# Folding the transforms over d a second time in a spectral filter with a gated MLP on one Trainium2 core

## The chip, the cores and the metric

The kernel runs on one core of a Trainium2 chip. The metric is the device time of one execution in microseconds, lower is better; it is the median over the runs of the same program.

## What is computed

```python
def _A_ref(x, w_r, w_i):                       # x: 1 x 2048 x 576
    X = jnp.fft.rfft2(x, axes=(-2, -1))        # 2048 x 289 complex
    X = X * (w_r + 1j * w_i)
    return jnp.fft.irfft2(X, s=(S, D), axes=(-2, -1))

def _B_ref(x, w_gate, w_up, w_down):           # F = 4608
    g = jnp.einsum("bsd,df->bsf", x, w_gate)
    u = jnp.einsum("bsd,df->bsf", x, w_up)
    return jnp.einsum("bsf,fd->bsd", _sigmoid(g) * u, w_down)

xn = _layernorm(x, axis=-1)
return x + _A_ref(xn, A_w_r, A_w_i) + _B_ref(xn, B_w_gate, B_w_up, B_w_down)
```

Everything is fp32. The change concerns the part `_A_ref`, and in it the transform over d (576 wide) and its inverse.

## The kernel before

TensorE multiplies fp32 operands that are split in two parts, a high and a low one (`split`: ScalarE copies the high part, VectorE subtracts it), as three products: high by high, low by high, high by low. Every product is one instruction that loads 128 columns of weights and streams up to 512 columns past them.

The gated MLP fills the whole time: `unit` and `plain` make the hidden values (`prod`, L636, 7 products of 512 columns per call into the banks `pA`, `pB`, `pE`), and `down` and `seven` multiply them with `w_down` (`po`, L743, and `ps`, L834, six products of 288 columns for half of a pair of banks). VectorE adds `po` and `ps` to the sums `acc` and `qs`. All of the smaller work takes pairs of PSUM banks from one tag, `pp`, with two buffers.

The spectral part is cut in three phases of 16 pieces, which run as generators beside the second half of the MLP: `begin` says at which step (one call of `prod` of the second pass) a piece starts, and at each step every active piece goes on to its next `yield`.

- `phase1b(t)`, begun every 4.1 steps from step 0, is the transform over d and the first half of that over the rows. Its 128 rows come transposed as `xs`, both halves of d in 2 x 3 blocks of 128 rows: two blocks of 128 and one with the last 32 rows four times. VectorE folds d once: the second half of d is stored backwards, and `eo` holds the differences (L465) and, after the mean is taken off (L466), the sums (L467) of the two halves, 288 values each. ScalarE makes the high parts `fh` (L470), VectorE the low ones `fl` (L471) and those of the last 32 rows, which lie in a part of `fh` (L473). Two steps later come the products `pd`: for sums and differences seven each, of 290 columns (`NQ`; L483). `ah` and `al` are the two parts of `pd`, and `pa` are the next products.
- `phase2(i)` multiplies by the filter.
- `phase3(t)` goes back: products `py`, transposes `pz` (six, of 128 columns), and the inverse transform over d, `pe`, again seven products for each half, of 288 columns (L594). VectorE adds the sum and the difference of the two halves of `pe` to the two halves of a row of the output (L598 to L601).

The products of the transform over d, before:

```python
for e in range(2):
    steps = []
    for k in range(2):
        steps += [(fh[:, e, k, :], cf[:, e, k, :]), (fl[:, e, k, :], cf[:, e, k, :]), (fh[:, e, k, :], cf[:, e, 2 + k, :])]
    steps.append((fh[:KR, e, KT, :], cf[:KR, e, 4, :]))
    for n, (l, r) in enumerate(steps):
        nc.tensor.matmul(pd[:, e, :NQ], l, r, start=n == 0, stop=n == len(steps) - 1)
```

A scheduler orders the instructions of each engine before the run, so this order is fixed; those marked with `keep_in_program_order` or `placed` are held to the order of the program.

Of the kernel before, what the change touches and what calls it, by code (L numbers as in the profile page):

```python
# [9 lines left out]
F32 = mybir.dt.float32  # L10
# [3 lines left out]
OP = mybir.AluOpType  # L14
# [10 lines left out]
FR = HD + 1 - 2 * P  # L25
# [18 lines left out]
KOF = np.array(list(range(1, 257)) + [0] + list(range(257, 289)))  # L44
# [19 lines left out]
def _constants():  # L64
    out = {}

    mid = np.arange(HD) - (D - 1) / 2
    ang = 2 * np.pi * mid[:, None] * KOF[None, :] / D
    t = np.zeros((P, 2, 5, NQ), np.float32)
    for e, v in ((0, np.cos(ang)), (1, -np.sin(ang))):  # L70
        m = np.zeros((HD, NQ))
        m[:, :KD] = v
        m[:, KD - 1 if e == 0 else KT * P] = 0.0
        hi, lo = _split(m)
        for part, w in ((0, hi), (1, lo)):
            t[:, e, 2 * part] = w[:P]
            t[:, e, 2 * part + 1] = w[P:2 * P]
        t[:KR, e, 4] = np.concatenate([hi[2 * P:], hi[2 * P:], lo[2 * P:]])
    out["cf"] = t.reshape(P, 10 * NQ)
# [26 lines left out]

    a = np.where((KOF == 0) | (KOF == HD), 1.0, 2.0)[:, None] / (D * S)
    co, si = a * np.cos(ang.T), a * np.sin(ang.T)
    co[KD - 1] = 0.0
    si[KT * P] = 0.0  # L110
    t = np.zeros((P, 2, 5, HD), np.float32)
    for e, m in ((0, co), (1, si)):
        hi, lo = _split(m)
        for part, w in ((0, hi), (1, lo)):
            t[:, e, 2 * part] = w[:P]
            t[:, e, 2 * part + 1] = w[P:2 * P]
        t[:3 * FR, e, 4] = np.concatenate([hi[2 * P:], hi[2 * P:], lo[2 * P:]])
    out["di"] = t.reshape(P, 10 * HD)
# [4 lines left out]
COLS = np.concatenate([np.arange(HD), np.arange(HD, D)[::-1]])  # L123
# [3 lines left out]
def _layout(x, w_r, w_i, w_gate, w_up, w_down):  # L127
# [4 lines left out]
    v = np.stack([w_r, w_i])[:, :, KOF].reshape(2, N1, N2 // 2, 2, KD).transpose(2, 1, 0, 3, 4)  # L132
    v = np.broadcast_to(v[:, None], (N2 // 2, 2, N1, 2, 2, KD))
    x = x.reshape(S, D)[ROWS][:, COLS]
    xt = x.reshape(NT, P, 2, HD)[..., ks].reshape(NT, P, 2, KT + 1, P).transpose(0, 4, 2, 3, 1)
    xg = xt[TPP:].reshape(2, TPC, P, 2, KT + 1, P).transpose(0, 3, 2, 4, 1, 5).reshape(2, 2, P, (KT + 1) * CW)
    lay = {"x": x.reshape(NT, P, D), "xt": xt.reshape(NT, P, 2 * (KT + 1) * P), "xg": xg, "ri": v.reshape(N2 // 2, P, 4 * KD),
# [11 lines left out]
def spectral_glu_kernel(ctx: ExitStack, tc: tile.TileContext, x, xt, xg, ri, w_in, w_down, out):  # L149
# [302 lines left out]
    def phase1b(t):  # L452
        pool, cf = R["pool"], R["cf"]
        xs = pool.tile([P, 2, KT + 1, P], F32, tag="xs", name=f"xs{t}", bufs=2)
        nc.sync.dma_start(xs.rearrange("p h k s -> p (h k s)"), xt[t])
# [769 lines left out]
```

## Time and profile before

| | us |
|---|---|
| median of 3 runs (1419.65 to 1420.62) | 1419.71 |
| the profiled execution | 1421.62 |
| its span, first to last instruction | 1419.8 |
| TensorE busy with products | 1405.9 (99%) |
| weight loads, which overlap the products | 1235.9 (87%) |
| VectorE busy | 1112.5 (78%) |
| ScalarE busy | 640.6 (45%) |
| mean granted clock of TensorE | 0.997 |

Busy time is a union over the span. A product's own duration in the trace runs from its start until its last result is out, and the next one begins well before that; what a product costs in a stream is the distance from one to the next, which the chain of waits shows as the time of a group divided by its count.

### The profile page before, as it was taken

What the parts mean: (1) busy time and instruction counts of PE and PEld (TensorE: products, weight loads), DVE (VectorE), ACT (ScalarE), POOL (GpSimd) and SP (SyncE); (2) the same over time, 40 slices, a digit from 0 to 9 for tenths busy, and PEclk for the clock granted to TensorE, in tenths of its full rate; (3) what the DMA queues carried; (4) which work ended last, traced back from release to release, by engine and by line L of the source; (5) the groups of instructions that cost most, each with busy time, mean ns of one, the idle gap of its engine ahead of it and who ended that gap; (6) DMA issues with size and microseconds to landing.
All of it is one profiled execution on the core that took longest, in us unless ns stands there. A gap on an engine that the chain in (4) does not pass through costs nothing. (4 is left out here: it accounts for less than half of the span.)

```text
span 1419.8 us, 20725 instructions
## 1 busy us (share of the span) xinstructions
PE 1405.9 (99%) x7883; PEld 1235.9 (87%) x7883; DVE 1112.5 (78%) x1722; ACT 640.6 (45%) x1035; POOL 3.3 (0%) x5
## 2 busy tenths in 40 slices
PE   8999999999999999999999999999999999999998
PEld 6888888888888888888888888888888889999897
DVE  6988888888888888789466888877878877766784
ACT  5644444444444443444235444434545534434431
POOL 0000000000000000000000000000000000000000
PEclk9999999999999999999999999999999999999999
DMA  6498677777777776675767777778888787766643
GB/s 250 181 329 308 256 267 262 270 263 270 263 269 263 269 263 247 242 254 176 270 217 234 224 234 223 217 245 267 275 269 272 236 290 221 247 215 204 195 126 84
DMA packets 130899, 343.10 MB, mean 242 GB/s; under 512 B 12176, under 2 KB 51632, under 8 KB 125936
## 3 DMA queue, kind: packets, MB, share of 16 engines
q1 hardware_dynamic: 129872, 340.47, 71.0%
q8 instruction: 62, 1.02, 0.3%
q10 hardware_dynamic: 928, 1.31, 0.3%
q14 instruction: 37, 0.30, 0.1%
HBM read 205.60 MB, written 136.13 MB: 241 GB/s over the span
## 5 line engine op out<-in xcount | busy, mean ns | idle before, releaser
L636 PE MATMUL pB<-X,w 128*128 128x512 f32 x1484 | 379.9, 393 | 0.0
L636 PEld LDWEIGHTS pB<-X,w 128*128 128x128 f32 x1484 | 268.0, 188 | 49.6 <-ACT v L700 1.3
L636 PE MATMUL pE<-X,w 128*128 128x512 f32 x1064 | 271.8, 392 | 0.5 <-DVE y L701 0.5
L636 PE MATMUL pA<-X,w 128*128 128x512 f32 x1008 | 261.4, 395 | 1.2 <-DVE X L445 0.8
L636 PEld LDWEIGHTS pE<-X,w 128*128 128x128 f32 x1064 | 193.2, 188 | 35.4 <-DVE y L701 1.0
L636 PEld LDWEIGHTS pA<-X,w 128*128 128x128 f32 x1008 | 184.5, 190 | 35.4 <-DVE X L445 1.7
L743 PE MATMUL po<-wd,hh 128*128 128x288 f32 x1216 | 210.8, 295 | 0.0
L834 PEld LDWEIGHTS ps<-wf,hs 128*128 128x128 f32 x1260 | 188.9, 188 | 17.9 <-ACT qs L842 0.9
L834 PE MATMUL ps<-wf,hs 128*128 128x288 f32 x1260 | 202.0, 295 | 0.4 <-ACT qs L842 0.4
L743 PEld LDWEIGHTS po<-wd,hh 128*128 128x128 f32 x1216 | 184.2, 188 | 11.8 <-ACT hh L726 0.4
L747 DVE TENSOR_TENSOR acc<-acc,po 128x576 f32<-128x576 f32 x168 | 125.7, 749 | 67.3 <-PE po L743 66.8
L240 ACT ACTIVATE w<-raw 128x768 fp32r<-128x768 f32 (+1 forms) x106 | 100.8, 952 | 93.1 <-PE pE L636 36.5
L743 PE MATMUL po<-wd,hl 128*128 128x288 f32 x608 | 128.7, 293 | 0.0
L844 DVE TENSOR_TENSOR qs<-qs,ps 128x576 f32<-128x576 f32 x112 | 84.1, 751 | 28.4 <-PE ps L834 27.4
L743 PEld LDWEIGHTS po<-wd,hl 128*128 128x128 f32 x608 | 98.7, 189 | 0.0
L701 DVE TENSOR_TENSOR y<-v,pE 128x512 f32<-128x512 f32 x68 | 46.7, 686 | 52.2 <-ACT v L700 51.3
L844 DVE TENSOR_TENSOR acc<-acc,ps 128x576 f32<-128x576 f32 x90 | 67.5, 750 | 23.3 <-PE ps L834 22.6
L242 DVE TENSOR_TENSOR w<-raw,w 128x512 fp32r<-128x512 f32 (+1 forms) x106 | 81.8, 772 | 3.2 <-ACT w L240 2.9
L721 DVE TENSOR_TENSOR y<-y,g 128x1024 f32<-128x1024 f32 x67 | 81.9, 1222 | 3.1
L770 ACT ACTIVATE hs<-y 128x512 fp32r<-128x512 f32 x105 | 64.8, 628 | 38.2 <-DVE y L721 14.6
L704 ACT ACTIVATE g<-pB 128x512 f32<-128x512 f32 x68 | 40.7, 598 | 89.9 <-PE pB L636 89.9
L700 ACT ACTIVATE v<-pB 128x512 f32<-128x512 f32 x68 | 40.6, 598 | 71.0 <-PE pB L636 70.7
(175 smaller groups left out, 1609.0 us busy)
## 6 DMA issues: line engine op xcount, KB each, us to landing
w<-wsp SPq DMA_DIRECT2D x246, 320.0 KB, 3.5
wsp<-w SPq DMA_DIRECT2D x34, 2240.0 KB, 7.8
raw<-in_w SPq DMA_DIRECT2D x34, 768.0 KB, 9.7
wdsp<-wd SPq DMA_DIRECT2D x36, 576.0 KB, 4.6
wf<-tsp SPq DMA_DIRECT2D x60, 288.0 KB, 3.9
wf<-wdsp SPq DMA_DIRECT2D x45, 288.0 KB, 3.9
std<-in_wd SPq DMA_DIRECT2D x36, 288.0 KB, 5.5
ri<-in_ri SPq DMA_DIRECT2D x16, 578.0 KB, 5.3
```

What stands on the lines that cost most here:

```text
L240: placed(nc.scalar.activation(o[:, :, :3, :], src, AF.Copy))
L242: placed(nc.vector.tensor_tensor(o[:, :, 3:, :], src[:, :, :KT, :], f32(o[:, :, :KT, :]), op=OP.subtract))
L636: nc.tensor.matmul(bank, w[:, sw, :], X[:, x, sx, :], start=start and j == 0, stop=stop and j == len(STEPS) - 1, skip_group_check=skip)
L700: nc.scalar.activation(v[:, 1], bank["B"], AF.Copy)
L701: nc.vector.tensor_tensor(y[:, 1], v[:, 1], bank["E"], op=OP.add)
L704: nc.scalar.activation(g[:, 1], bank["B"], AF.Sigmoid)
L721: nc.vector.tensor_tensor(y, y, g, op=OP.mult)
L743: nc.tensor.matmul(pd[:, b, :HD], h[i], w[k][b], start=g == 0 and n == 0, stop=g == G - 1 and n == 2)
L747: nc.vector.tensor_tensor(a, a, pd[:, :, :HD], op=OP.add)
L770: nc.scalar.activation(hs[:, 0], src, AF.Copy)
L834: nc.tensor.matmul(pd[:, i, :HD], h[:, a, m], w[:, b], start=q == 0, stop=q == 2)
L844: nc.vector.tensor_tensor(o, o, pd[:, :, :HD], op=OP.add)
```

## The change

The transform over d is folded a second time. With the first fold, sums serve the cosines and differences the sines. Now each of them is folded again about the middle of its half: sums and differences of quarters of d (144 values) serve even and odd frequencies apart. The columns of d are ordered by quarters (`COLS`), the frequencies by odd ones first (`KOF`), and they are padded from 289 to 290 with one empty frequency.

In `phase1b`, `xs` comes as 2 x 2 x 2 blocks (the last 16 rows of a quarter eight times), the first fold works on 512 columns instead of 384, and six instructions of 128 columns make the second one, two of them with a sign per partition, `sg`. The products have one quarter each: per half, one product of 290 columns for the remainders of both quarters and six of 144 or 146 columns. ScalarE's high parts and VectorE's low ones cover as many elements as before.

In `phase3` the products `pe` have the same form, one of 288 columns and six of 144, and VectorE joins the quarters with five instructions instead of four. The tables `cf` and `di` shrink, to 128 x 1740 for `cf` from 128 x 2900.

```diff
-        eo = pool.tile([P, 2, KT + 1, P], F32, tag="eo", name=f"eo{t}")
-        tc.keep_in_program_order(nc.vector.tensor_tensor(eo[:, 1], xs[:, 0], xs[:, 1], op=OP.subtract))
-        nc.vector.scalar_tensor_tensor(xs[:, 0], mb.unsqueeze(1).to_broadcast([P, KT + 1, P]), -2.0, xs[:, 0], op0=OP.mult, op1=OP.add)
-        nc.vector.tensor_tensor(eo[:, 0], xs[:, 0], xs[:, 1], op=OP.add)
-        fh = pool.tile([P, 2, KT + 1, P], F32R, tag="fh", name=f"fh{t}")
-        fl = pool.tile([P, 2, KT, P], F32R, tag="fl", name=f"fl{t}")
+        od = pool.tile([P, 2, 2 * P], F32, tag="od", name=f"od{t}")
+        tc.keep_in_program_order(nc.vector.tensor_tensor(od, xs[:, 0], xs[:, 1], op=OP.subtract))
+        ev = xs[:, 0].rearrange("p j (k s) -> p (j k) s", s=P)
+        nc.vector.scalar_tensor_tensor(ev, mb.unsqueeze(1).to_broadcast([P, 4, P]), -2.0, ev, op0=OP.mult, op1=OP.add)
+        nc.vector.tensor_tensor(xs[:, 0], xs[:, 0], xs[:, 1], op=OP.add)
+        eo = pool.tile([P, 2, 3, P], F32, tag="eo", name=f"eo{t}")
+        for e, v in ((0, xs[:, 0]), (1, od)):
+            for c, op in ((1 - e, OP.add), (e, OP.subtract)):
+                nc.vector.tensor_tensor(eo[:, e, c], v[:, 0, :P], v[:, 1, :P], op=op)
+            nc.vector.scalar_tensor_tensor(eo[:, e, 2], v[:, 1, P:], sg, v[:, 0, P:], op0=OP.mult, op1=OP.add)
+        fh = pool.tile([P, 2, 3, P], F32R, tag="fh", name=f"fh{t}")
+        fl = pool.tile([P, 2, 2, P], F32R, tag="fl", name=f"fl{t}")
         nc.scalar.activation(fh, eo, AF.Copy)
...
         pd = pair(f"pd{t}")
         for e in range(2):
-            steps = []
-            for k in range(2):
-                steps += [(fh[:, e, k, :], cf[:, e, k, :]), (fl[:, e, k, :], cf[:, e, k, :]), (fh[:, e, k, :], cf[:, e, 2 + k, :])]
-            steps.append((fh[:KR, e, KT, :], cf[:KR, e, 4, :]))
-            for n, (l, r) in enumerate(steps):
-                nc.tensor.matmul(pd[:, e, :NQ], l, r, start=n == 0, stop=n == len(steps) - 1)
+            nc.tensor.matmul(pd[:, e, :NQ], fh[:KR, e, 2, :], cf[:KR, e, 2, :], start=True, stop=False, skip_group_check=True)
+            for c, o in ((0, slice(0, HQ)), (1, slice(HQ, NQ))):
+                for n, (v, i) in enumerate(((fh, 0), (fl, 0), (fh, 1))):
+                    nc.tensor.matmul(pd[:, e, o], v[:, e, c, :], cf[:, e, i, o], start=False, stop=n == 2, skip_group_check=True)
...
         pe = pair(f"pe{t}")
         for e in range(2):
-            steps = []
+            nc.tensor.matmul(pe[:, e, :HD], zr[:3 * FR, e, :], dr[:3 * FR, e, :], start=True, stop=False, skip_group_check=True)
             for k in range(2):
-                steps += [(zh[:, k, e, :], di[:, e, k, :]), (zl[:, k, e, :], di[:, e, k, :]), (zh[:, k, e, :], di[:, e, 2 + k, :])]
-            steps.append((zr[:3 * FR, e, :], di[:3 * FR, e, 4, :]))
-            for n, (l, r) in enumerate(steps):
-                nc.tensor.matmul(pe[:, e, :HD], l, r, start=n == 0, stop=n == len(steps) - 1)
+                o = pe[:, e, (k + 1 + e) % 2 * HQ:((k + 1 + e) % 2 + 1) * HQ]
+                for n, (l, i) in enumerate(((zh, 0), (zl, 0), (zh, 1))):
+                    nc.tensor.matmul(o, l[:, k, e, :], di[:, e, k, i, :], start=False, stop=n == 2, skip_group_check=True)
         od = pool.tile([P, HD], F32, tag="od", name=f"od{t}")
         nc.scalar.activation(od, pe[:, 1, :HD], AF.Copy)
-        lo, up = a[:, :HD], a[:, HD:]
-        nc.vector.tensor_tensor(lo, lo, od, op=OP.subtract)
-        nc.vector.tensor_tensor(lo, lo, pe[:, 0, :HD], op=OP.add)
-        nc.vector.tensor_tensor(up, up, od, op=OP.add)
-        nc.vector.tensor_tensor(up, up, pe[:, 0, :HD], op=OP.add)
+        V = pool.tile([P, 2, 2, HQ], F32, tag="ev", name=f"ev{t}")
+        for i, op in ((0, OP.add), (1, OP.subtract)):
+            nc.vector.tensor_tensor(V[:, i].rearrange("p a q -> p (a q)"), pe[:, 0, :HD], od, op=op)
+        w = a.rearrange("p (s v q) -> p s v q", s=2, v=2)
+        nc.vector.tensor_tensor(w, w, V[:, :, 0].unsqueeze(1).to_broadcast([P, 2, 2, HQ]), op=OP.add)
+        for i, op in ((0, OP.add), (1, OP.subtract)):
+            nc.vector.tensor_tensor(w[:, i], w[:, i], V[:, :, 1], op=op)
```

The scheduler's order of TensorE at tile 4 of the first transform, in the kernel before, from the second half of `ps2_0` into `pd4` (a name's number counts tiles, and `ps2_1_0` is the first half of the second product of round 2):

```order
L834 MATMUL ps2_0_1_7007<-wf2_0_6832,hs2_0_6900 128x288 x6
L636 MATMUL pB42_6950<-X_66,w38_6102 128x512 x7
L834 MATMUL ps2_1_0_7025<-wf2_1_6898,hs2_1_6971 128x288 x6
L483 MATMUL pd4_7038<-cf_6396,fh4_6989 128x290
L636 MATMUL pA42_6949<-X_66,w38_6102 128x512 x3
L483 MATMUL pd4_7038<-cf_6396,fl4_6990 128x290
L483 MATMUL pd4_7038<-cf_6396,fh4_6989 128x290 x2
L483 MATMUL pd4_7038<-cf_6396,fl4_6990 128x290
L483 MATMUL pd4_7038<-cf_6396,fh4_6989 128x290 x3
L483 MATMUL pd4_7038<-cf_6396,fl4_6990 128x290
```

The same place in the changed kernel:

```order
L853 MATMUL ps2_0_1_7044<-wf2_0_6855,hs2_0_6930 128x288 x6
L655 MATMUL pB42_6980<-X_66,w38_6102 128x512 x7
L853 MATMUL ps2_1_0_7062<-wf2_1_6928,hs2_1_7001 128x288 x6
L655 MATMUL pA42_6979<-X_66,w38_6102 128x512 x7
L655 MATMUL pB42_6980<-X_66,w38_6102 128x512 x3
L495 MATMUL pd4_7075<-cf_6396,fh4_7026 128x290
L498 MATMUL pd4_7075<-cf_6396,fh4_7026 128x144
L498 MATMUL pd4_7075<-cf_6396,fl4_7027 128x144
L498 MATMUL pd4_7075<-cf_6396,fh4_7026 128x144
L498 MATMUL pd4_7075<-cf_6396,fh4_7026 128x146
L498 MATMUL pd4_7075<-cf_6396,fl4_7027 128x146
L498 MATMUL pd4_7075<-cf_6396,fh4_7026 128x146
```

The products `pd4` have moved behind seven products of `pA42` and three of `pB42`, and their first one now reads the remainder rows, which are made last. The second half of `pd4` repeats this form.

VectorE at the same tile, before:

```order
L844 TENSOR_TENSOR qs_6448<-qs_6448,ps2_0_0_6962 128x576
L465 TENSOR_TENSOR eo4_6985<-xs4_6858 128x384
L771 TENSOR_TENSOR hs2_1_6971<-y41_6729,hs2_1_6971 128x512
L466 SCALAR_TENSOR_TENSOR xs4_6858<-mb4_6860,xs4_6858 128x384
L771 TENSOR_TENSOR hs2_2_7034<-y41_6729,hs2_2_7034 128x512
L467 TENSOR_TENSOR eo4_6985<-xs4_6858 128x384
L844 TENSOR_TENSOR qs_6448<-qs_6448,ps2_0_1_7007 128x576
L808 TENSOR_TENSOR y41_6729<-y40_6482,y41_6729 128x512
L471 TENSOR_TENSOR fl4_6990<-eo4_6985,fh4_6989 128x512
L473 TENSOR_TENSOR fh4_6989<-eo4_6985,fh4_6989 32x2x128
L844 TENSOR_TENSOR acc_163<-acc_163,ps2_1_0_7025 128x2x288
```

And in the changed kernel:

```order
L863 TENSOR_TENSOR qs_6450<-qs_6450,ps2_0_0_6992 128x576
L476 TENSOR_TENSOR od4_7015<-xs4_6888 128x512
L790 TENSOR_TENSOR hs2_1_7001<-y41_6752,hs2_1_7001 128x512
L478 SCALAR_TENSOR_TENSOR xs4_6888<-mb4_6890,xs4_6888 128x512
L483 TENSOR_TENSOR eo4_7019<-od4_7015 128x128
L479 TENSOR_TENSOR xs4_6888<-xs4_6888 128x512
L483 TENSOR_TENSOR eo4_7019<-od4_7015 128x128
L483 TENSOR_TENSOR eo4_7019<-xs4_6888 128x128 x2
L484 SCALAR_TENSOR_TENSOR eo4_7019<-xs4_6888,sg_6398 128x128
L484 SCALAR_TENSOR_TENSOR eo4_7019<-od4_7015,sg_6398 128x128
L863 TENSOR_TENSOR qs_6450<-qs_6450,ps2_0_1_7044 128x576
L863 TENSOR_TENSOR acc_163<-acc_163,ps2_1_0_7062 128x2x288
```

The block that makes `eo4` has grown from three instructions to nine, with one `hs` among them. The addition of `ps2_1_0`, which stood behind `fl4` and the remainder rows of `fh4`, now stands ahead of them, as that of `ps2_0_1` did already.

## Rows read from the trace of the kernel before

**Rows 1.** Busy time by stage: us, TensorE, its loads, VectorE, ScalarE, GpSimd, clock, DMA.

```profile
720.00:960.00 240.00, 238.40 (x1334) 206.19 (x1333) 190.94 (x312) 117.42 (x204) 0.00 (x0) 1.00 0.75 231
...
1160.00:1400.00 240.00, 239.99 (x1432) 216.73 (x1431) 169.85 (x275) 95.64 (x199) 0.00 (x0) 1.00 0.64 197
```

**Rows 2.** Chain that ended last, 791 to 806 us: start, us, what.

```profile
791.95 1.60 PE pE L636 x7
793.54 0.80 PE ps L834 x6
...
795.63 1.75 PE pd L483 x13
```

**Rows 3.** The same chain, 1171 to 1180 us.

```profile
1171.48 0.44 PE pz L577 x4
1171.92 0.15 PE pz L580 x2
...
1174.51 1.86 PE pe L594 x14
```

**Rows 4.** Timeline of weight loads, 1171.8 to 1172 us: start, us, instruction.

```profile
1171.84 0.30 PEld L636 LDWEIGHTS pB<-X,w 128*128 128x128 f32 x2
```

**Rows 5.** Weight loads, a group of the page: count, busy us, mean ns.

```profile
L636 PEld LDWEIGHTS pB<-X,w 128*128 128x128 f32 x1484 | 268.0, 188 | 49.6 <-ACT v L700 1.3
```

**Rows 6.** VectorE by line, 724 to 958 us: count, busy us, mean ns, idle before.

```profile
L492 DVE SCALAR_TENSOR_TENSOR al<-pd,rstd,ah 64x290 fp32r<-64x290 f32 x64 | 33.2, 519 | 19.5 <-ACT ah L491 18.1
L771 DVE TENSOR_TENSOR hs<-y,hs 128x512 fp32r<-128x512 f32 x40 | 26.8, 685 | 1.0 <-ACT hs L770 0.7
...
L465 DVE TENSOR_TENSOR eo<-xs 128x384 f32<-128x384 f32 x16 | 8.9, 553 | 0.2
L466 DVE SCALAR_TENSOR_TENSOR xs<-mb,xs 128x384 f32<-128x384 f32 x16 | 8.9, 553 | 0.2
L467 DVE TENSOR_TENSOR eo<-xs 128x384 f32<-128x384 f32 x16 | 8.8, 552 | 0.1
...
L473 DVE TENSOR_TENSOR fh<-eo,fh 32x256 fp32r<-32x256 f32 x16 | 6.6, 415 | 0.5
```

**Rows 7.** Waits, 724 to 958 us: who for whom, us, times, longest.

```profile
DVE al L492 <- ACT ah L491: 18.1, 18, 2.9
...
DVE y L701 <- ACT v L700: 13.4, 5, 7.2
...
DVE acc L844 <- PE ps L834: 5.9, 8, 2.1
DVE qs L844 <- PE ps L834: 5.6, 6, 1.6
...
PEld pa L498 <- DVE al L492: 3.7, 8, 0.6
...
PEld pd L483 <- ACT fh L470: 1.2, 3, 0.5
PEld pd L483 <- DVE fl L471: 1.0, 4, 0.3
```

**Rows 8.** Instructions by line, 800 to 1420 us: count, busy us, mean ns.

```profile
L844 DVE TENSOR_TENSOR qs<-qs,ps 128x576 f32<-128x576 f32 x108 | 81.1, 750 | 28.3 <-PE ps L834 27.4
...
L470 ACT ACTIVATE fh<-eo 128x768 fp32r<-128x768 f32 x10 | 8.5, 847 | 9.1 <-DVE eo L467 9.0
...
L209 DVE TENSOR_TENSOR rp<-py,rp 128x66 fp32r<-128x66 f32 x16 | 3.6, 226 | 5.3 <-ACT rp L208 4.9
...
L599 DVE TENSOR_TENSOR fin<-fin,pe 128x288 f32<-128x288 f32 x8 | 3.6, 446 | 0.0
```

**Rows 9.** Timeline of VectorE, 791 to 797.5 us.

```profile
791.99 0.75 DVE L844 TENSOR_TENSOR acc<-acc,ps 128x576 f32<-128x576 f32 x1
792.66 0.55 DVE L467 TENSOR_TENSOR eo<-xs 128x384 f32<-128x384 f32 x1
```

More of the change, by code (lines that the diff above doesn't have):

```diff
@@ L24 @@
 HD = D // 2
-FR = HD + 1 - 2 * P
+HQ = HD // 2
+FR = NQ - 2 * P
 CW = 512
@@ L41 @@
 U1, U2, U3 = (0, 4.1), (76, 4.1), (151, 4.5)
-KOF = np.array(list(range(1, 257)) + [0] + list(range(257, 289)))
+KOF = np.array(list(range(1, HD, 2)) + [0] + list(range(0, HD + 1, 2)))
+PAD = HD // 2
+QTR = np.arange(HQ)
+FREQ = np.arange(NQ) != PAD
+ODD = np.arange(NQ) < PAD
 def _split(m):
@@ L65, in _constants @@
     out = {}
[L67 to L73, printed above, removed]
-        hi, lo = _split(m)
[L75 to L79, printed above, removed]
+    ang = 2 * np.pi * (QTR[:, None] + 0.5) * KOF[None, :] / D
+    t = np.zeros((P, 2, 3, NQ), np.float32)
+    for e, m in ((0, np.cos(ang)), (1, np.sin(ang))):
+        m = np.where(FREQ & (KOF != (HD, 0)[e]), m, 0.0)
+        hi, lo = _split(m)
+        t[:, e, 0], t[:, e, 1] = hi[:P], lo[:P]
+        even, odd = ~ODD, ODD
+        both = []
+        for v in (hi, hi, lo):
+            both += [v[P:] * w.astype(np.float32) for w in ((even, odd) if e == 0 else (odd, even))]
+        t[:KR, e, 2] = np.concatenate(both)
+    out["cf"] = t.reshape(P, 6 * NQ)
+    out["sg"] = np.where(np.arange(P) % REM < REM // 2, 1.0, -1.0).astype(np.float32)[:, None]
     s1 = np.arange(N1)
@@ L104, in _constants @@
     out["bm"] = b.reshape(P, 4 * P)
[L107 to L112, printed above, removed]
-        hi, lo = _split(m)
[L114 to L118, printed above, removed]
+    a = np.where((KOF == 0) | (KOF == HD), 1.0, 2.0)[:, None] / (D * S) * FREQ[:, None]
+    ang = 2 * np.pi * KOF[:, None] * (QTR[None, :] + 0.5) / D
+    t = np.zeros((P, 2, 2, 2, HQ), np.float32)
+    r = np.zeros((P, 2, HD), np.float32)
+    for e, m in ((0, a * np.cos(ang)), (1, a * np.sin(ang))):
+        m[KOF == (HD, 0)[e]] = 0.0
+        hi, lo = _split(m)
+        for k, rows in enumerate((slice(0, P), slice(NQ - P, NQ))):
+            t[:, e, k, 0], t[:, e, k, 1] = hi[rows], lo[rows]
+        h, l = np.zeros((2, FR, HD), np.float32)
+        for s, v in ((h, hi), (l, lo)):
+            v = v[P:NQ - P]
+            o = ODD[P:NQ - P]
+            s[o, (1 - e) * HQ:(2 - e) * HQ] = v[o]
+            s[~o, e * HQ:(e + 1) * HQ] = v[~o]
+        r[:3 * FR, e] = np.concatenate([h, h, l])
+    out["di"] = np.concatenate([t.reshape(P, 8 * HQ), r.reshape(P, 2 * HD)], 1)
     out["id"] = np.eye(P, dtype=np.float32)
     return out
-COLS = np.concatenate([np.arange(HD), np.arange(HD, D)[::-1]])
+COLS = np.concatenate([HD - 1 - QTR, HD + QTR, QTR, D - 1 - QTR])
 ROWS = np.arange(S).reshape(N1, N2).T.ravel()
@@ L507, in phase2 @@
         nc.sync.dma_start(x2, sc1.rearrange("(p kl) n -> p kl n", kl=N2)[:, kl:kl + 2])
-        w = pool.tile([P, 2, 2, KD], F32, tag="ri", name=f"ri{i}", bufs=2)
+        w = pool.tile([P, 2, 2, NQ], F32, tag="ri", name=f"ri{i}", bufs=2)
         nc.sync.dma_start(w.rearrange("p a j n -> p (a j n)"), ri[i])
@@ L606, in stage1 @@
         pool = room("1")
-        R["cf"] = cf = pool.tile([P, 2, 5, NQ], F32R, name="cf")
-        load_r(cf, con["cf"].rearrange("p (e k n) -> p e k n", e=2, k=5))
+        R["cf"] = cf = pool.tile([P, 2, 3, NQ], F32R, name="cf")
+        load_r(cf, con["cf"].rearrange("p (e k n) -> p e k n", e=2, k=3))
+        R["sg"] = sg = pool.tile([P, 1], F32, name="sg")
+        nc.sync.dma_start(sg, con["sg"])
         yield
@@ L616, in stage2 @@
         zl = pool.tile([P, 2, NQ], F32R, name="zl")
-        for z in (zh, zl):
-            nc.vector.memset(f32(z)[:, :, KD:], 0.0)
         R["zz"] = [(zh, zl)]
@@ L623, in stage3 @@
         pool = room("3")
-        R["di"] = di = pool.tile([P, 2, 5, HD], F32R, name="dit")
-        load_r(di, con["di"].rearrange("p (e k n) -> p e k n", e=2, k=5))
+        R["di"] = di = pool.tile([P, 2, 2, 2, HQ], F32R, name="dit")
+        R["dr"] = dr = pool.tile([P, 2, HD], F32R, name="drt")
+        load_r(di, con["di"][:, :8 * HQ].rearrange("p (e k i q) -> p e k i q", e=2, k=2, i=2))
+        load_r(dr, con["di"][:, 8 * HQ:].rearrange("p (e n) -> p e n", e=2))
         yield
```

42 lines of the change are left out of this document (22 added, 20 removed).

## The prediction

> **What bounds the kernel now.** I read the busy time by stage first. The changed products lie in two of the three stretches of [rows 1]: the transform into frequencies in 720 to 960 us, the one back in 1160 to 1400 us. TensorE is busy for 238.40 and 239.99 of 240 us there, at a granted clock of 1.00, so its stream sets the end, and a microsecond less of it is a microsecond less of the kernel as long as nothing else comes late. The second reading of [rows 1] is who could: VectorE has 190.94 of 240 us in the first stretch and 169.85 in the second. The first has 49 us to spare, the second 70.
>
> Next, the chain of waits, which here is TensorE's own order and so gives a price per product. In [rows 2], 13 products `pd` of 290 columns take 1.75 us, 0.135 each; six of 288 take 0.80 us, 0.133 each; seven of 512 take 1.60 us, 0.229 each. In [rows 3], the 14 products `pe` of one tile take 1.86 us, 0.133 each. All have a weight load of 128 columns ahead of them.
>
> **What the change removes on TensorE.** A tile keeps 14 products in `pd` and 14 in `pe`. Two of each stay at full width, twelve have 144 or 146 columns. So 12 x 2 x 16 = 384 products are halved, and no weight load goes away. The price of a half product is not in the trace, so I bound it.
>
> Below, if columns alone counted: from 288 to 512 columns the pitch grows by 0.229 - 0.133 = 0.096 us for 224, 0.00043 us a column; 144 fewer leave 0.071 us. Above, by the weight load. The nearest rows are the transposes, 128 columns each with a load of its own: four take 0.44 us [rows 3], 0.110 each. In [rows 4], two loads with nothing between them end 0.30 us after the first began; one lasts 0.188 us [rows 5], so the second began 0.11 us after the first. I take it that loads do not come closer than that, whatever is streamed. A half product streams for less, and as each needs its load I take 0.110 us.
>
> The saving is (0.134 - 0.110) x 384 = 9.2 us, half in each stretch. At 0.071 it would be 24 us. At 0.134 it would be nothing.
>
> The Trainium skill states both sides. In "TensorE: Matmul & The Clock Gate", section "Back-to-back issue gap", the warm gap of one matmul is N/2.4 + 2.5 ns, 62.5 ns for 144 columns, an estimate which would make the sum 23 us. Its section "LDWEIGHTS (loading the stationary operand)" gives P/1.2 ns, 107 ns for 128 columns, and so 10 us. Of the two the trace agrees with the load (0.110 against 107 ns); for the gap it has 0.229 us at 512 columns where the first gives 215.8 ns.
>
> **What it adds on VectorE, first transform.** Three instructions of 384 columns go (553, 553 and 552 ns, together 1.66 us, [rows 6]). Three of 512 come (685 ns each, as `hs` in [rows 6]), four of 128, and two of 128 with a scalar per partition. A row of 66 columns takes 226 ns and one of 288 takes 446 ns [rows 8], 0.99 ns a column, so 128 columns are 287 ns. The scalar is priced by `al`, 519 ns for 290 columns [rows 6], 71 ns above that line: 358 ns. New: 3 x 0.685 + 4 x 0.287 + 2 x 0.358 = 3.92 us. That is 2.26 us more a tile, 36 us over 16. An instruction can begin 0.08 us before the one ahead ends (792.66 against 791.99 + 0.75, [rows 9]), which for six more of them gives back up to 0.48 us a tile: 28 us is the other end. I take 32. VectorE then has 223 us in the first stretch, which is itself to shrink to 235.4.
>
> So the cover is nearly gone, and the place where it shows is tile 4, whose rows are in the section on the change. From the end of the product `ps2_0_0`, VectorE has its addition (0.750, [rows 8]), the new block (3.92), `hs` (0.685), two additions (1.50), `fl` (0.685) and the remainder rows of `fh` (0.415): 7.96 us, or 7.4 with overlap at half of the seams. ScalarE's `fh` (0.847, [rows 8]) fits beside the two additions. TensorE has until `pd4`: six of `pa` (0.80), 6 x 0.229, `ps` (0.80), seven (1.60), `ps` (0.80), seven (1.60), three (0.69): 7.66 us. It finds `fl` and `fh` between 0.26 us early and 0.30 us late. In the kernel before, `pd` waits for them for 1.2 and 1.0 us in all [rows 7]. I take 0.2 us a tile, 3.2 us, and keep 0 to 0.4, 0 to 6.4 us. The order already answers to this: `pd4` now stands ten products of 512 columns behind `ps2_1_0`, where its first one stood right behind it before. Behind a waiting `pd` stand the products of the main matmuls, which nobody else needs sooner.
>
> **What it adds in the second transform.** Four instructions of 288 columns (446 ns, [rows 8]) become four of 288 and one of 576 (0.750): 0.75 us a tile, 12 us, and VectorE has 182 of 235.4 us. No work of TensorE waits for its results before the final sums, and `pe`'s bank is read out after two instructions instead of four. Nothing, then; without the cover it would be 12 us.
>
> **The rest.** `xt` grows from 384 to 512 KB a tile; of TensorE's own waits in the first stretch the longest are for `al`, `fh` and `fl` [rows 7], and none is for a transfer. The tables shrink. Frequencies are padded from 289 to 290, some ns for each of a few instructions. Nothing for these together.
>
> **Sum.** -9.2 + 3.2 = -6.0 us. The profiled execution took 1421.62 us (span 1419.8 and 1.8 around it), so it would take 1415.6. The median of the runs is 1.9 us lower, 1419.71, and becomes 1413.7. With a stall of 0 to 6.4 us that is 1410.5 to 1416.9.
>
> **Rivals.**
> *VectorE sets the pace of the first stretch.* Of its 49 us of idle time, 43.0 have a name: 18.1 for `ah`, 13.4 for `v`, 11.5 for `ps` [rows 7]. Against this rival: a late engine finds its inputs ready, and those waits shrink. For it: `al` and `ah` take turns, so some stay. If half stay, 223 + 21.5 = 244.5 us stand against 235.4, the stall is 9.1 us, and the time is 1419.6, no change. All of them would give 1441. From 57% on (24.4 us) the kernel is slower by over 0.2%.
> *A short stream is no cheaper, or dearer.* This ends on the other side. No product with fewer than 288 columns is in the trace, only transposes, and fp32 operands could pass at fewer than one column per cycle in a short stream. Against it: the transposes of 128 columns, two of them with the same fp32r type, take 0.15 us a pair [rows 3]; but a transpose is no product. The place is the 384 half products, the point is a pitch of 0.134 us, from which nothing is saved. If a half product took as long as one of 512, (0.229 - 0.134) x 384 = 36 us are lost, and with the stall it is some 1456 to 1459 us.
> *Loads are pulled ahead, columns count.* Then 24 us less and 3.2 more, 1399 us. Against it stand 0.110 us a transpose and the loads of [rows 4]; for it, only that transposes are no products either. [...] The Trainium skill's same page, section "The mechanism" (Part 3), says a load overlaps a running matmul only in another row group; the loads here use all rows, and yet a product of 288 columns with its load takes 0.133 us in [rows 3], less than 0.110 for the load and its stream one after the other, so the measurement decides.
>
> **How the numbers follow.** Small stall, load-bound products: 0.62, at 1413.7. VectorE sets the pace: 0.18, of which 0.12 within 0.2% and 0.06 slower. Short stream dear: 0.13. Columns count: 0.07. A difference under 0.2% (2.8 us) is about what a measurement of this kernel cannot tell from none. Faster is then 0.62 + 0.07 = 0.69, the same 0.12, slower 0.19. The range leaves out the dear stream and the cheap one, 0.20, and takes in the pace up to a few us of loss: 1409.8 to 1423.
>
> **What would show it.** In the changed trace, a `pe` tile should take 2 x 0.133 + 12 x 0.110 = 1.59 us in the chain, not 1.86; a weight load should start every 0.11 us in it. 1.12 us a tile would mean columns count, 1.86 or more the dear stream. The VectorE work up to 960 us should be about 223 us, and waits of `pd` for `fl` and `fh` some 5 us in all, against 2.2 before. I would be wrong if the sum of TensorE's waits in that stretch came out above 9 us, or if those of `ps` for its bank appeared.

## The result, and the profile after

The changed kernel takes 1426.29 us (median of 5 runs, 1426.01 to 1428.03) against 1419.99 for the kernel before on the same chip (5 runs): 1.0046 times as long, 95% interval 1.0035 to 1.0057. It is slower by 6.3 us where 6.0 us less were forecast. The profiled execution took 1426.01 us, its span 1424.2.

The page's busy times over the whole span, and the busy time by stage, which answers to [rows 1] (columns: stretch, its length, then busy us and instructions of TensorE, weight loads, VectorE, ScalarE and GpSimd, granted clock, DMA share, GB/s):

```profile
PE 1400.8 (98%) x7883; PEld 1223.1 (86%) x7883; DVE 1151.4 (81%) x1832; ACT 641.2 (45%) x1035; POOL 3.3 (0%) x5
```

```profile
720.00:960.00 240.00, 229.95 (x1288) 191.90 (x1287) 212.35 (x397) 114.05 (x197) 0.00 (x0) 1.00 0.73 226
1160.00:1400.00 240.00, 238.87 (x1443) 213.69 (x1443) 184.75 (x296) 97.36 (x202) 0.00 (x0) 1.00 0.66 201
```

In the first stretch TensorE has gone from 238.40 to 229.95 of 240 us: it now stands still for 10 us, at the same granted clock of 1.00. In the last stretch it is busy for 1.1 us less. So most of the loss is in the first transform.

The products themselves did what was forecast. The chain of waits at a tile of the inverse, which answers to [rows 3] (start, us, what):

```profile
1177.75 0.44 PE pz L593 x4
...
1180.79 0.14 PE pe L605
1180.92 0.63 PE pe L609 x6
1181.55 0.18 PE pe L605
1181.73 0.63 PE pe L609 x6
```

Six half products take 0.63 us, 0.105 each, and a tile 1.58 us where it took 1.86. The timeline shows the starts in the tile's second half (start, us, instruction):

```profile
1181.39 0.34 PE L605 MATMUL pe<-drt,z3r 102*128 102x288 f32 x1
1181.56 0.23 PE L609 MATMUL pe<-dit,z3h 128*128 128x144 f32 x1
1181.63 0.27 PE L609 MATMUL pe<-dit,z3l 128*128 128x144 f32 x1
1181.74 0.39 PE L609 MATMUL pe<-dit,z3h 128*128 128x144 f32 x2
1181.97 0.28 PE L609 MATMUL pe<-dit,z3l 128*128 128x144 f32 x1
```

The first half product starts 0.17 us behind the remainder's product and the second 0.07 behind the first; from there on the distance is 0.11 us, that of the transposes. So 0.105 is a mean of six.

VectorE's new block, too, costs what was forecast. Its groups from 724 to 964 us, which answer to [rows 6] (line, operation, shape, count, then busy us in all and mean ns):

```profile
L479 DVE TENSOR_TENSOR xs<-xs 128x512 f32<-128x512 f32 x16 | 10.9, 684 | 0.0
L476 DVE TENSOR_TENSOR od<-xs 128x512 f32<-128x512 f32 x15 | 10.3, 690 | 0.3
L478 DVE SCALAR_TENSOR_TENSOR xs<-mb,xs 128x512 f32<-128x512 f32 x15 | 10.3, 688 | 0.2
L483 DVE TENSOR_TENSOR eo<-od 128x128 f32<-128x128 f32 x32 | 9.1, 283 | 0.0
...
L484 DVE SCALAR_TENSOR_TENSOR eo<-od,sg 128x128 f32<-128x128 f32 x16 | 5.5, 344 | 0.0
```

What is new is seen in TensorE's waits from 725 to 962 us, for products and then for weight loads (what waited and for whom: us in all, times, longest):

```profile
PE ps L853 <- DVE acc L863: 4.8, 4, 1.5
PE ps L853 <- DVE qs L863: 1.8, 2, 1.6
...
PE pd L495 <- DVE fh L490: 0.2, 1, 0.2
```

```profile
PEld ps L853 <- DVE acc L863: 7.5, 7, 1.9
...
PEld ps L853 <- DVE qs L863: 4.1, 8, 2.0
PEld pd L495 <- issue: 2.5, 9, 0.6
```

In the kernel before, in the same window, `ps` waited as follows, again for products and then for weight loads:

```profile
PE ps L834 <- ACT qs L842: 0.4, 1, 0.4
```

```profile
PEld ps L834 <- ACT qs L842: 0.9, 1, 0.9
...
PEld ps L834 <- DVE acc L844: 0.8, 2, 0.4
```

`ps` waits for the addition (L863) that empties its bank pair; `pd` hardly waits for VectorE's block by name (what its loads wait for in the 2.5 us of "issue" the profile does not show). One such wait, at tile 4 of the first transform. VectorE's timeline (start, us, instruction, shape, count):

```profile
782.62 0.69 DVE L790 TENSOR_TENSOR hs<-y,hs 128x512 fp32r<-128x512 f32 x1
783.35 0.69 DVE L827 TENSOR_TENSOR y<-y,y 128x512 f32<-128x512 f32 x1
784.08 0.69 DVE L827 TENSOR_TENSOR y<-y 128x512 f32<-128x512 f32 x1
784.74 0.69 DVE L790 TENSOR_TENSOR hs<-y,hs 128x512 fp32r<-128x512 f32 x1
785.35 0.69 DVE L827 TENSOR_TENSOR y<-y,y 128x512 f32<-128x512 f32 x1
785.95 0.68 DVE L790 TENSOR_TENSOR hs<-y,hs 128x512 fp32r<-128x512 f32 x1
786.55 0.69 DVE L827 TENSOR_TENSOR y<-y,y 128x512 f32<-128x512 f32 x1
787.16 0.51 DVE L507 SCALAR_TENSOR_TENSOR al<-pd,rstd,ah 64x290 fp32r<-64x290 f32 x1
787.59 0.74 DVE L863 TENSOR_TENSOR acc<-acc,ps 128x576 f32<-128x576 f32 x1
```

and TensorE's:

```profile
784.38 1.00 PE L853 MATMUL ps<-wf,hs 128*128 128x288 f32 x6
785.22 1.08 PE L655 MATMUL pB<-X,w 128*128 128x512 f32 x4
786.13 0.84 PE L655 MATMUL pA<-X,w 128*128 128x512 f32 x3
788.38 1.06 PE L853 MATMUL ps<-wf,hs 128*128 128x288 f32 x6 [1.40 <-DVE acc L863]
```

The products that the addition needs are done at 785.4. It begins at 787.59, since work for the next rounds (`hs`, sums of `y`) and an `al` stand ahead of it in VectorE's queue. The next `ps` needs that bank pair and waits 1.40 us, with everything behind it.

For the experiments I sum TensorE's lost time from the starts of its products: the distance from each product to the next, less the price of the first (0.227 us for 512 columns, 0.133 for 288 and 290, 0.1055 for half products and transposes), put down to the tile of the later one. The first stretch runs from the first `ps` to the first `pb`, the last from the first `py` to the last `pe`.

| us | first stretch | its products | lost | ahead of `ps`, `pd`, `pa` | last stretch | lost |
|---|---|---|---|---|---|---|
| before | 230.4 | 219.8 | 10.6 | 1.7, 1.6, 3.8 | 223.7 | 2.9 |
| after | 239.1 | 214.4 | 24.6 | 14.8, 2.3, 5.5 | 221.7 | 6.0 |

The products give 5.4 and 5.1 us back, 10.5 in all; the first stretch loses 14.0 us more than before, the last 3.1. These prices are means: they make a `pe` tile 1.53 us where the chain has 1.58, so 0.8 us of what the last stretch loses is the distance behind the remainder's product and no wait. By the chain the inverse gets 16 x 0.28 = 4.5 us back.

### The profile page after: what moved, and what is told of

Read it like the earlier page. It is cut to its first block, busy times and chain, and to the rows that moved or that the text cites. A ratio compares the mean times of both kernels' runs of the same rounds, so it can differ in the third digit from the quotient of the medians.

```text
span 1424.2 us, 20824 instructions
## 1 busy us (share of the span) xinstructions
PE 1400.8 (98%) x7883; PEld 1223.1 (86%) x7883; DVE 1151.4 (81%) x1832; ACT 641.2 (45%) x1035; POOL 3.3 (0%) x5
## 5 line engine op out<-in xcount | busy, mean ns | idle before, releaser
L853 PEld LDWEIGHTS ps<-wf,hs 128*128 128x128 f32 x1260 | 185.3, 188 | 28.6 <-DVE acc L863 7.5
L863 DVE TENSOR_TENSOR qs<-qs,ps 128x576 f32<-128x576 f32 x112 | 83.8, 750 | 24.5 <-PE ps L853 23.4
L863 DVE TENSOR_TENSOR acc<-acc,ps 128x576 f32<-128x576 f32 x90 | 67.2, 749 | 17.4 <-PE ps L853 16.7
L790 DVE TENSOR_TENSOR hs<-y,hs 128x512 fp32r<-128x512 f32 x105 | 71.0, 686 | 2.1 <-ACT hs L789 1.4
```

The lines of the kernel that those rows point to most:

```text
L790: return lambda: nc.vector.tensor_tensor(hs[:, 1], src, f32(hs[:, 0]), op=OP.subtract)
L853: nc.tensor.matmul(pd[:, i, :HD], h[:, a, m], w[:, b], start=q == 0, stop=q == 2)
L863: nc.vector.tensor_tensor(o, o, pd[:, :, :HD], op=OP.add)
```

## The experiments

**The parts of the change.** My first theory was the stall by VectorE's lateness: its longer block makes TensorE wait. The rivals were the narrow products themselves. The first two runs undo one of the transforms.

```diff
 # e1_inverse_alone: the first transform as before
-        for e in range(2):
-            nc.tensor.matmul(pd[:, e, :NQ], fh[:KR, e, 2, :], cf[:KR, e, 2, :], start=True, stop=False, skip_group_check=True)
...
+            for n, (l, r) in enumerate(steps):
+                nc.tensor.matmul(pd[:, e, :NQ], l, r, start=n == 0, stop=n == len(steps) - 1)
 # e2_first_alone: pe and the sums behind it as before
```

> The second fold in the inverse transform alone; the first transform has its old products and its old VectorE work (same frequencies, same output). Theory A, the loss comes from VectorE's longer block in the first transform: the first stretch is as before, the inverse keeps what it gained in the changed kernel (some 2 us), 1416.5 to 1418.5 us. Rival B, narrow products disturb the stream wherever they stand: no gain, 1420 or more.

> The second fold in the first transform alone, the inverse as before. Theory A: the whole loss and a little more, 1420 + 8 to 9, so 1427.5 to 1429.5 us, with waits of ps for acc and qs on TensorE. Rival B: about half of the loss, 1422 to 1424.

Measured 1418.23 us (ratio 0.9985, 0.9976 to 0.9994) and 1428.85 (1.0059, 1.0044 to 1.0074). Both are as the first theory has it. The inverse alone gains 1.8 us against the 1420.02 of the kernel before in these runs: 5.1 us by its products, less 3.1 in waits. The first transform alone loses 8.8. The next two split the first transform.

```diff
 # e3_narrow_products_alone: the changed products behind the old VectorE work
-        od = pool.tile([P, 2, 2 * P], F32, tag="od", name=f"od{t}")
...
+        eo = pool.tile([P, 2, KT + 1, P], F32, tag="eo", name=f"eo{t}")
+        tc.keep_in_program_order(nc.vector.tensor_tensor(eo[:, 1], xs[:, 0], xs[:, 1], op=OP.subtract))
...
 # e4_block_alone: the changed VectorE work ahead of products of 290 columns
-                    nc.tensor.matmul(pd[:, e, o], v[:, e, c, :], cf[:, e, i, o], start=False, stop=n == 2, skip_group_check=True)
+                steps += [(fh[:, e, k, :], cf[:, e, 0, :]), (fl[:, e, k, :], cf[:, e, 0, :]), (fh[:, e, k, :], cf[:, e, 1, :])]
```

> The narrow products in both transforms with VectorE's work as it was before in both (three instructions of 384 columns, four of 288 for the sums), so that the output is not the transform. Theory A: the saving appears whole, 9 to 10 us, 1410 to 1412.5 us. Rival B: the gain stays below 4 us.

> VectorE's nine instructions in the first transform with the 14 wide products of before on what they give, inverse as before; the output is not the transform. Theory A1, TensorE waits because sums of ps come late, and these waits add to its own work: some 13 us more than before, 1431 to 1434 us, 4 to 6 us above the kernel with the first transform alone. Theory A2, VectorE's total work sets the length of the stretch, whatever TensorE has to do: the same time as with the first transform alone, within 1.5 us.

Measured 1422.28 (1.0014, 1.0004 to 1.0023) and 1422.58 (1.0015, 1.0005 to 1.0025). Both expectations of my theory fell. The block alone, 3.88 us a tile, loses 12.5 us in the first stretch, 1.9 more than before, though VectorE is busy for 218 of 240 us. The narrow products, with VectorE's old instructions, lose 21.2 us, 8.9 of them ahead of `ps`. So the narrow products bring the waits for VectorE, which does the same work as before, but in an order that the scheduler chose anew. By the starts in the trace, the seven latest additions of `ps` begin 1.7 to 3.1 us after their products there, against 1.3 to 1.8 us in the kernel before; the mean is about the same, 0.63 and 0.59 us. Lateness alone does not decide, though: behind the block alone the additions are on the mean as late as in the changed kernel (1.17 and 1.19 us), yet `ps` loses 4.1 us there and 14.8 in the changed kernel. Second theory: the order is the cause.

**The order by itself.** The same instructions can be held to another kernel's order. At the end of the program each engine's instructions (TensorE, VectorE, ScalarE) are chained. This adds no instruction to them, and TensorE's loads wait for 243 to 247 semaphores in the changed kernel with a chain and for 244 without:

```diff
+    for engine, order in ORDER.items():      # places in program order
...
+        for a, b in zip(row, row[1:]):
+            tc.add_manual_dep(b, a.name, how, reason="order")
```

`ORDER` is read off a kernel that has the same instructions and is ordered by the scheduler. For the changed kernel that is a twin whose half products are wide (`pd` is shown, `pe` is treated alike):

```diff
-                    nc.tensor.matmul(pd[:, e, o], v[:, e, c, :], cf[:, e, i, o], start=False, stop=n == 2, skip_group_check=True)
+                    nc.tensor.matmul(pd[:, e, :NQ], v[:, e, c, :], cf[:, e, i], start=False, stop=n == 2, skip_group_check=True)
```

> The narrow products alone, as in the run before with VectorE's old instructions (the output is not the transform), but TensorE, VectorE and ScalarE each issue their instructions in the order that they have in the kernel before; only that order differs from the earlier run of the narrow products (1422.28 us, 21.2 us lost by TensorE in the first stretch). Theory A (order): the ordering pass places the additions that free the banks of `ps` later when it sees narrow products, and TensorE then waits for them; with the old order the loss falls to 10 to 13 us and the time is 1411 to 1414 us. Theory B (hardware): narrow products themselves make TensorE arrive early and wait whatever the order; 1421 to 1423 us.

> The kernel before with nothing changed but the order: TensorE, VectorE and ScalarE issue in the order that the kernel with narrow products alone has. The products stay wide. Theory A (order): TensorE reaches each tile of `ps` behind a `pd` only about 0.27 us later than with narrow products, so most of the waits for the additions of `ps` appear here too, 4 to 9 us of them: 1424 to 1429 us. Theory B (the narrow products are the cause, not the order): 1419.5 to 1420.8 us, as before.

> The changed kernel complete, its output the reference's, with TensorE, VectorE and ScalarE in the order that a twin of it gets in which the 24 half products of a tile's two transforms are wide (288 and 290 columns). Theory A (order): the first stretch loses about 13 us instead of 24.6 (the run of VectorE's block with wide products lost 12.5), and with product times of 214.4 us it lasts 227 to 229 us; the last stretch 219 to 222; in all 1413 to 1417 us, faster than the kernel before by 0.2 to 0.5%. Theory B (VectorE's block and narrow products together, whatever the order): 1424 to 1428 us.

> The changed kernel complete, with VectorE alone in the order of the wide twin; TensorE and ScalarE are ordered anew around it. If it is VectorE's queue that carries the loss: within 1.5 us of the run in which all three engines have the twin's order (1413 to 1418 us). If the place of the tiles in TensorE's own queue carries it: over 1420 us. Theory B: 1424 to 1428 us.

Measured 1426.15 (1.0040, 1.0025 to 1.0056), 1429.49 (1.0062, 1.0048 to 1.0075), 1418.04 (0.9981, 0.9973 to 0.9990) and 1424.11 (1.0024, 1.0014 to 1.0035).

The second is the plainest: not an instruction differs from the kernel before, and it is 9.0 us slower than that kernel's 1420.5 in these runs. TensorE's waits there:

```profile
PE ps L838 <- DVE qs L848: 2.5, 2, 1.7
PE ps L838 <- DVE acc L848: 2.2, 3, 1.0
PE pa L502 <- DVE al L496: 1.8, 2, 1.0
```

They are waits of the same kind as with the narrow products, with wide ones. The changed kernel gains 8 us by its twin's order, in the first stretch (17.1 lost, 7.0 of it ahead of `ps`) and in the last (3.9). That is 1 us above the range of theory A and well below that of theory B. VectorE's order alone, with the other two engines ordered anew around it, gives about a quarter of it, so VectorE's queue by itself does not carry the loss. The first run lies above the ranges of both theories, and its waits say why:

```profile
PE pd L494 <- DVE fh L489: 11.9, 10, 1.4
```

The waits ahead of `ps` are nearly gone (2.2 us lost), but the first of the narrow products reads the remainder, VectorE's last result, where in the kernel before that product is the seventh; the order was made for the latter. A run below has it last, as there.

**Moving single instructions.** If late additions are the whole matter, they can be moved up. The rule: on VectorE, in the first stretch, each addition of `ps` goes ahead of the instructions that in the kernel's trace began after the addition's products were done.

```diff
 # e9, e10, e11: ORDER["DVE"], first stretch
-  hs, y, y, hs, y, hs, y, al, acc<-ps2_1_1
+  hs, y, y, hs, acc<-ps2_1_1, y, hs, y, al
 # e12: the remainder's product last, with the narrow products alone in the order of the kernel before
+            nc.tensor.matmul(pd[:, e, :NQ], fh[:KR, e, 2, :], cf[:KR, e, 2, :], start=False, stop=True, skip_group_check=True)
```

> The changed kernel complete, its output the reference's. TensorE and ScalarE keep the order that they have in it; on VectorE, in the first stretch alone, each addition of a tile of `ps` is moved ahead of those instructions that in the trace of the changed kernel began after the addition's products were done: 38 additions, by 151 places in all, mostly ahead of parts of the new block. No instruction is added or left out. Theory A (the additions stand behind the block in VectorE's queue and keep the banks of `ps`): TensorE's waits in front of `ps` fall from 14.8 us to 3 to 6, the waits of `pd` and `pa` grow by 1 to 3 together, 1415 to 1420 us. Theory B (VectorE has too much work, so the wait only moves to `pd` and `pa`): 1423 to 1428 us.

> The changed kernel complete, in the order of the wide twin, which alone gave 1418.04 us with 17.1 us lost in the first stretch, 7.0 of them in front of `ps`; and here too the additions of `ps` in that stretch are moved up on VectorE by the same rule (37 additions, 129 places). Theory A: `ps` loses 2 to 3 us, the stretch 12 to 14, the time is 1412.5 to 1416 us. Theory B: the wait moves to `pd` and `pa`, 1417 to 1419 us.

> The kernel before with nothing but the same rule applied to its own trace (29 additions of `ps`, by 44 places). It loses only 1.7 us in front of `ps`. If the queue of VectorE costs only where the new block stands in it: 1418.5 to 1420.5 us, no change or a little faster. If such an order would have helped the kernel before as much as the changed one (a gain of 5 us or more): under 1415.5 us, and the loss would not belong to the change.

> The narrow products alone in the order of the kernel before, as in the run that took 1426.15 us (the output is not the transform), with one thing mended: there the first product of a `pd` tile read the remainder, which VectorE's last instruction before it writes, so `pd` waited 15.7 us; here the remainder's product is the last of the seven, as it is in the kernel before. Theory A (order): `pd` loses 1 to 4 us, `ps` about 2, the first stretch 11 to 14 us in all, and the time is 1411 to 1415 us. Theory B (narrow products cost their saving in any order): 1420 us or more.

Measured 1440.34 (1.0141, 1.0127 to 1.0155), 1431.26 (1.0079, 1.0065 to 1.0093) and 1428.65 (1.0057, 1.0044 to 1.0071) for the moved additions: all three are slower than without the move, the kernel before too, and slower than either theory had them. The waits ahead of `ps` did fall (14.8 to 6.2, 7.0 to 4.4, 1.7 to 1.0 us), but `pa` lost 16.0, 11.6 and 7.0 us where it had lost 5.5, 5.2 and 3.8, and `pd` 6 to 7 us in each. On VectorE in the first of them, against 8.1 us for the first of these rows and 0.2 for the last in the changed kernel:

```profile
DVE al L511 <- ACT ah L510: 16.7, 20, 2.5
DVE acc L867 <- PE ps L857: 5.1, 6, 2.1
DVE fl L492 <- ACT fh L491: 3.9, 10, 0.9
```

With the additions moved, VectorE waits longer for ScalarE. So "the additions are late" is what the wait looks like; what costs the time is the order as a whole. No run holds a kernel to its own order by a chain, but the changed kernel has now been chained to three orders, at 1418.04, 1431.26 and 1440.34 us, in programs that differ in nothing else. The fourth run, 1412.82 us (0.9949, 0.9936 to 0.9963), is what the run of 1426.15 us was meant to be: the narrow products alone lose 12.8 us in the first stretch, 2.2 more than the kernel before, and 7.1 us are gained. So narrow products do not cost their saving by themselves.

**Work or order.** The complete kernel still lost 17.1 us in its twin's order. Either VectorE has too much to do, or the remainder's place costs, or the order is still not good. The first run below moves the remainder's product to the end, in the twin's order. The next two have a joined block as well, 2.69 us a tile instead of 3.88 (two instructions of 0.686 us, two of 0.419, one of 0.480), in their own order and in their twin's. The last leaves the mean's subtraction out of the kernel before.

```diff
-        nc.vector.scalar_tensor_tensor(ev, mb.unsqueeze(1).to_broadcast([P, 4, P]), -2.0, ev, op0=OP.mult, op1=OP.add)
...
+        for o, op in ((q[:, 1:4:2], OP.add), (q[:, 0:5:4], OP.subtract)):
+            nc.vector.tensor_tensor(o, fo[:, :, 0, :P], fo[:, :, 1, :P], op=op)
+        nc.vector.scalar_tensor_tensor(eo[:, :, 2], fo[:, :, 1, P:], sg, fo[:, :, 0, P:], op0=OP.mult, op1=OP.add)
```

> The changed kernel complete, its output the reference's, with the remainder's product moved to the end of the seven in each half of a `pd` tile, in the order of its wide twin (this order without the move gave 1418.04 us). If the wait of `pd` for the remainder is the rest of the loss: `pd` loses under 1 us instead of 2.4, `ps` and `pa` fall with it, 1414 to 1416.5 us. If it is VectorE's amount of work: 1416.5 to 1419 us.

> The changed kernel with less work in VectorE's block, its output still the reference's: the subtraction of the mean is left out (it reaches only frequency 0, whose column of the table is set to zero), and the six folds of quarters are three instructions of twice the size. By the measured prices of the block (0.69 us for 512 columns, 0.28 and 0.35 for 128) that is 3.9 us a tile down to about 2.7, so 19 us less VectorE work in the first stretch, near the kernel before. The remainder's product is last, and the order is the kernel's own. If VectorE's amount of work is the cause: the stretch loses 11 to 14 us and the time is 1411 to 1415 us in any order. If the order is the greater part: the waits of `ps` stay at 6 us or more, 1417 to 1422 us.

> The same kernel with the joined block, in the order of its own wide twin. Either theory (the amount of work, or the order) has its cause taken away here, so both expect the first stretch to lose 11 to 14 us, as with the narrow products alone in the right order (12.8), and the time to be 1411 to 1414.5 us, the fastest of all. If it is 1417 us or more, something else costs, such as the narrow products beside the block.

> The kernel before with the subtraction of the mean left out in the same way (column of frequency 0 set to zero; the output is the reference's): 16 instructions of 0.69 us and 16 loads fewer, 11 us less VectorE work in the first stretch. If VectorE's amount of work already cost the kernel before something: 1414 to 1418 us. If it did not: 1419 to 1421 us, give or take an order that falls out otherwise.

In the first three, other than expected, the output is not the transform: the second half of a bank starts the bank's sums anew (as in the fourth run above; without that start, in the last run below, the output is the transform). The number and the sizes of the instructions are as stated. Measured 1415.58 (0.9964, 0.9950 to 0.9978), 1427.23 (1.0042, 1.0028 to 1.0056), 1413.26 (0.9949, 0.9936 to 0.9963) and 1418.03 (0.9983, 0.9974 to 0.9992). The second is 5 us above even the range for the order. The second and third have the same instructions. Their first stretch, own order and then twin's:

```profile
720.00:960.00 240.00, 225.93 (x1283) 194.53 (x1281) 196.89 (x331) 113.44 (x196) 0.00 (x0) 0.99 0.73 226
```

```profile
720.00:960.00 240.00, 236.41 (x1350) 204.01 (x1349) 205.97 (x346) 120.50 (x207) 0.00 (x0) 1.00 0.76 237
```

In its own order VectorE is busy for 196.89 of 240 us, little more than in the kernel before, and TensorE still loses 25.4 us. The amount of VectorE's work is not the cause of that loss. The order is: 14 us between these two. The remainder's place cost about 2.5 us (1418.04 to 1415.58; the two intervals just overlap). The last run is faster than the kernel before by 0.17%; its order was made anew as well, so whether less work or another order gives that was not parted.

**Why the order comes out so.** The programs of twins of the changed kernel with half products of different widths were compared place by place. Between 248 and 255 columns VectorE's order differs in 24 places and TensorE's in 112; between 255 and 256 it is 341 and 800; between the kernel's own widths and 255 it is 130 and 445. So at 256 columns something seems to change in what the scheduler takes a product to cost. The next run is the changed kernel in the order from just beyond that step (`pe` is treated like `pd`); the last is the joined block with its sums mended.

```diff
 # e17: the twin that gives the order
+                    nc.tensor.matmul(pd[:, e, :256], v[:, e, c, :], cf[:, e, i, :256], start=False, stop=n == 2, skip_group_check=True)
 # e18
-                    ... start=n == 0, stop=False
+                    ... start=n == 0 and c == 0, stop=False
```

> The changed kernel complete, its output the reference's, with TensorE, VectorE and ScalarE in the order of a twin whose half products have 256 columns, just beyond the step between 255 and 256 (the order of the twin with 288 and 290 columns gave 1418.0 us, the kernel's own with 144 and 146 gave 1426.3). If a wrong price under 256 columns makes the order bad: 1416 to 1420.5 us. If the order only worsens step by step as products get narrower, with no such price: 1420.5 to 1425 us.

> The kernel with the joined block in the order of its wide twin (1413.26 us), where the first product of the second half of a bank no longer starts the sums anew: only the first product of the bank does. In the runs with the remainder's product last that start was made in both halves, so that the columns of the first half lost their sums of three products; the number and the sizes of the instructions are the same. The output is the reference's now, and the time is 1412.5 to 1414.5 us, faster than the kernel before by 0.4 to 0.55%; over 1416 us if the sums had mattered to the time.

Measured 1413.88 (0.9956, 0.9943 to 0.9970) and 1413.35 (0.9954, 0.9941 to 0.9968). The first is the changed kernel, instruction for instruction, and 12.4 us faster than in its own order; it is below both of its ranges, on the side of the first. The order from 255 columns was not run, so that the step itself carries the time is argued. Its first stretch, the waits of `ps` from 725 to 962 us, and VectorE and TensorE at the place shown above:

```profile
720.00:960.00 240.00, 238.87 (x1344) 201.60 (x1343) 219.32 (x409) 120.15 (x207) 0.00 (x0) 1.00 0.78 240
```

```profile
PEld ps L857 <- DVE qs L867: 1.1, 4, 0.3
PEld ps L857 <- DVE acc L867: 1.1, 4, 0.4
```

```profile
783.13 0.69 DVE L831 TENSOR_TENSOR y<-y 128x512 f32<-128x512 f32 x1
783.79 0.69 DVE L794 TENSOR_TENSOR hs<-y,hs 128x512 fp32r<-128x512 f32 x1
784.40 0.51 DVE L511 SCALAR_TENSOR_TENSOR al<-pd,rstd,ah 64x290 fp32r<-64x290 f32 x1
784.83 0.74 DVE L867 TENSOR_TENSOR acc<-acc,ps 128x576 f32<-128x576 f32 x1
```

```profile
784.26 1.08 PE L659 MATMUL pB<-X,w 128*128 128x512 f32 x4
785.18 0.61 PE L659 MATMUL pA<-X,w 128*128 128x512 f32 x2
785.64 1.04 PE L857 MATMUL ps<-wf,hs 128*128 128x288 f32 x6
```

Three rows fewer stand ahead of the addition, and `ps` goes on after two products of 512 columns without a wait. Here TensorE is busy for 238.87 us and VectorE for 219.32 of 240: the stretch loses 14.2 us and the last one 3.8. With the joined block the time is 0.5 us less still, which is less than the spread of the runs. Both beat the kernel before and the changed one.

## Why the prediction was wrong

- **The price of a half product.** 0.110 us forecast from the transposes; measured 0.105 on the mean and 0.11 from the third of six on. A `pe` tile takes 1.58 us where 1.59 was forecast. That is 0.28 us less than before, and 9.0 us over 32 tiles if `pd` gains as much, against 9.2 forecast (the 10.5 of the table prices the distance behind the remainder's product as a loss). Right. By the Trainium skill's page "TensorE: Matmul & The Clock Gate", section "LDWEIGHTS (loading the stationary operand)", P/1.2 ns for a load of 128 columns is 107 ns, and the trace agrees with it (0.105 to 0.11 us). The 62.5 ns from the formula in the Trainium skill's section "Back-to-back issue gap" of that page is for an isolated matmul, as the section says itself, and is not seen in this stream. The dear short stream and the stream by columns fell with that, on the chip.
- **VectorE's block.** 3.92 us a tile forecast; the rows above give 0.690 + 0.688 + 0.684 + 4 x 0.283 + 2 x 0.344 = 3.88. Right. VectorE's 223 us up to 960 us were 212.35 in the changed kernel, whose first stretch was not over by then, and 219.32 in the order from the 256-column twin.
- **The stall, +3.2 us: the step that failed.** I counted only what `pd` waits for `fl` and `fh`, at tile 4, and went on with "The order already answers to this". `pd` lost 2.3 us against 1.6, 0.7 more and not 3.2; `ps`, whose waits I put at nothing, lost 14.8 against 1.7, 13.1 more. I had compared the two orders around `pd` alone and priced the stalls as if the rest of the order were as good as before. It was not: the same instructions in the order from the 256-column twin take 1413.88 us, and the difference to 1426.29, 12.4 us, is the scheduler's order. That 1413.88 is near my 1413.7 is in part luck: the first stretch loses 3.6 us more than before in that order, near my 3.2, but nearly all of it is ahead of `ps` (5.2 against 1.7) and little ahead of `pd` (2.3 again). Waits of `ps` for its bank, or over 9 us of waits in the stretch, stood among the signs of being wrong; both came.
- **The inverse, nothing lost.** The last stretch lost 3.1 us more than before in the kernel's own order and 0.9 in the order from the 256-column twin; some 0.8 us of either is no wait but the distance behind the remainder's product. The other 2 us of the 3.1 go with the order.
- **VectorE sets the pace.** Fell: 19 us less work for VectorE left 1427.23 us in the kernel's own order, and the whole block is carried at 1413.88 in another. As argued against this rival, the waits of a late engine shrink: 43.0 us of VectorE's idle time had a name before [rows 7]; the same three (`ah`, `v`, `ps`) come to 18.8 us in the changed kernel and to 9.8 in the order from the 256-column twin.

What the scheduler takes a narrow product to cost was not seen; that it is more than the measured 0.105 us is argued from the step at 256 columns. Why the order costs what it does, instruction by instruction, and why moved additions make VectorE wait longer for ScalarE, was not followed further.

## What to carry to other kernels

Where a scheduler fixes each engine's order before the run, a change of a few instructions' size is two changes: what the instructions cost, and what order they fall into; here the products gave 9 to 10.5 us back and the order alone cost 12.4. Run the old instructions in the new order and the new ones in an old order before blaming an engine's load: it costs a list of places, and the order of a twin may be kept if it is faster. Mending such an order one instruction at a time, by the waits of one trace, was slower in all three attempts here.

## What was unexpected on the chip

- One set of instructions took 1413.9, 1418.0, 1424.1, 1426.3, 1431.3 and 1440.3 us in six orders, at granted clocks of 0.997 to 0.998 in the profiled executions: 1.9%, without a transfer or a product more.
- VectorE busy for 219.32 of 240 us, 91%, left TensorE busy for 238.87; busy for 196.89 in another order (of the joined block), it left 225.93.
- Six products of 144 columns take 0.105 us each, and from the third on they start 0.11 us apart, like the transposes of 128 columns (0.110); one of 288 columns takes 0.133: half the columns are 21% less time.
